# One fused kernel of attention and two expert layers: what a slot's two arms hold, and how the second layer's routing sums are laid out

## The chip, the cores and the metric

The kernel runs on one core of one Trainium2 chip. Times are device microseconds of one execution. The metric is the median of several runs; before the change it is 712.32 us over 3 runs (710.05 to 712.72). The engines are TensorE (PE, with its weight loads shown apart as PEld), VectorE (DVE), ScalarE (ACT), GpSimd (POOL) and SyncE (SP), and each has a sequencer that takes its instructions in program order (shown as PEldq, DVEq and so on).

## The reference

Three steps in a row, all in fp32. The first is a gated linear attention over 64-row blocks (4 batches, 8 heads, 768 rows of 64), whose output is 3072 tokens of 512. Then come two layers of experts: of eight experts each token takes the one with the largest gate, computes relu(x w1) w2 with w1 512x1024 and w2 1024x512, and scales it by its softmax weight. The second layer skips tokens whose skip score is not positive, and adds its input.

```python
def moe(x, w_gate, bias, w1, w2):
    logits = x @ w_gate + bias
    e_idx = argmax(logits, 1)
    gate_w = softmax(logits)[arange(N), e_idx]
    for e in range(8):
        mask = e_idx == e
        out[mask] = gate_w[mask, None] * (maximum(x[mask] @ w1[e], 0) @ w2[e])
    return out
x1 = moe(attention(q, k, v, lam), ...)
do = x1 @ w_skip > 0
x2 = x1.copy(); x2[do] = x1[do] + moe(x1[do], ...)
```

## The kernel before, in words

Tokens are written to a table, grouped by expert, and worked on in slots of 256 rows (two blocks of 128). Every fp32 product with the experts' weights is made of three faster ones: weights and inputs are split into a high and a low part (`w1h`, `w1l`, `xth`, `xtl`, `hh`, `hl`), and three matmuls are added up. ACT rounds the high parts, DVE subtracts to get the low ones.

The first expert layer has 14 slots (`which` = 0, kk = 0 to 13), the second 10 (`which` = 1). Slot kk = 0 of each is written out by itself (`first1`, `first2`). `slot` (L861 on) makes the others, `rec` nests them: the first twelve slots of layer 1 always run, each later one stands in an If of its own (`more0_12` and so on, L922), and their Else arm is the passage to the second layer (`tail`, L909).

A slot does two products, which the code calls `layer1` and `layer2`; in this document "step n" is the n-th output part of either. `layer1` (L710) is x w1: eight steps f of 12 matmuls with 256 columns each, at L717 to L719; behind every second step ACT takes relu (L724) and DVE the low part (L725). `layer2(j)` (L753) is h w2 for block j: eight steps n of three matmuls with 512 columns each, at L758 to L760. Both take functions to call behind a step (`steps`, `hooks`), which is how smaller work is laid between. `trans_x` transposes the next slot's rows (L350, copies at L353, low part at L354). `split_next` splits the next slot's w1 if its expert differs (flag `fl` > 0), with ACT at L304 and DVE at L305, and reloads the raw buffer (`fl` > 1). `split_w2` does the same for w2 at the head of a slot (L310, L311). Which expert, which flag and whether a slot is full is read by each engine from a table into a register (L323).

A slot with more than 128 rows is full; in a half one only block 0 has rows. `slot` decides by one If (L892), whose two arms each hold the whole rest of the slot: the full arm `layer1`, `trans_x`, `split_next` and both blocks; the half arm `layer1_half` (L729; rows as weights, w1 as 512 moving columns, L736 to L738, then transposes back, L745), `trans_x`, and block 0 with `split_next` behind its step 5. In this data three slots are half: kk = 6 and 12 of layer 1 and kk = 7 of layer 2. Each slot but the last ones of layer 1 also issues a prefetch hint for the next slot's branch (`ahead`, L864).

While slot kk of layer 1 runs, the 256 results of slot kk - 1 are routed for the second layer (`router`, L661; also once in `first2`). `tr` transposes them (L669) into `x2t`. `la` (L672) multiplies them with the gate weights `wgp`: the 512 inputs are cut in four parts c, and each part's product goes, without accumulation, to another 32 rows of a PSUM tile, 256 tokens wide; ACT copies that to `lgs` (L675). `lg` (L677) adds the four parts and turns the result to tokens in rows, by two matmuls with a 0/1 matrix `sel` (L679). `rk` (L681 on, DVE) finds the chosen expert per token as a 0/1 row `oh` and sums per expert. `rb` (L694 on) ranks the tokens by two small matmuls with `tri` and `ones` (L136, L137), turns that into table rows on DVE (L140 to L157) and scatters on POOL. In a full slot these are the steps 1 (`tr`), 3 (`la`), 4 (`lg`, `rk`) and 6 (`rb`) of `layer1`. In a half slot `la` stands behind the second half of `layer1_half`, `lg` and `rk` behind its DVE work, and `rb` in block 0.

Of the kernel before, what the change touches and what calls it, by code (L numbers as in the profile page):

```python
# [18 lines left out]
P = 128  # L19
E = 8  # L20
# [15 lines left out]
def body(ctx: ExitStack, tc: tile.TileContext, qkv, cpk, w1, w2, out, dbg=None):  # L36
# [77 lines left out]
    def route_a(L, n, mask=None):  # L114
        m = rt.tile([P, 4], F32, tag="m", name="m")
        nc.vector.tensor_reduce(out=m[:, :n], in_=L, axis=AX.X, op=ALU.max)
        d = rt.tile([P, 4, E], F32, tag="d", name="d")
# [5 lines left out]
        oh = rt.tile([P, 4, E], BF16, tag="oh", name="oh")  # L123
# [515 lines left out]
    lgs = hp.tile([P, 2, P], F32, name="lgs")  # L639
    wgp = hp.tile([P, 4, 32], F32, name="wgp")  # L640
    sel = hp.tile([P, E + 1], F32, name="sel")
    plg = pmi[:, 256:512].rearrange("p (j t) -> p j t", j=2)
# [11 lines left out]
    def fill():  # L654
        nc.gpsimd.memset(wgp, 0.0)
        nc.gpsimd.tensor_copy(out=wgp[:, :, 0:E + 1], in_=wgt2)
        nc.gpsimd.tensor_tensor(out=sel, in0=ident[:, 0:E + 1], in1=ident[:, 32:33 + E], op=ALU.add)
        for i in (64, 96):
            nc.gpsimd.tensor_tensor(out=sel, in0=sel, in1=ident[:, i:i + E + 1], op=ALU.add)
        for t in (x2r[1][1], xgm[0], xgm[1]):  # L660
            nc.gpsimd.memset(t, 0.0)  # L661

    def router(ix, kk=None):
        box = []
# [7 lines left out]
        def la():  # L672
            for c in range(4):
                nc.tensor.matmul(plg[32 * c:32 * c + 32], wgp[:, c], x2t[:, c], start=True, stop=True)
            nc.scalar.copy(out=lgs, in_=plg)  # L675

        def lg():  # L677
            for j in range(2):
                nc.tensor.matmul(pmi[:, 16 * j:16 * j + E + 1], lgs[:, j], sel, start=True, stop=True)  # L679

        def rk():  # L681
            L = rt.tile([P, 2, 16], F32, tag="L2", name="L2")
            nc.vector.tensor_copy(out=L[:, :, 0:E + 1], in_=pmi[:, 0:32].rearrange("p (t e) -> p t e", e=16)[:, :, 0:E + 1])
# [4 lines left out]
            mask = rt.tile([P, 2], F32, tag="mask", name="mask")  # L688
            nc.vector.scalar_tensor_tensor(out=mask, in0=L[:, :, E], scalar=0.0, in1=pres, op0=ALU.is_gt, op1=ALU.mult)
            oh, ex = route_a(L[:, :, 0:E], 2, mask)  # L690
            route_s(oh, 2, 1)
            box[:] = (oh, ex, mask)

        def rb(cnt=None):  # L694
            oh, ex, mask = box
# [12 lines left out]
        return tr, la, lg, rk, rb  # L708
# [110 lines left out]
    def first2():  # L819
        la, lg, rk, rb = router(itl)[1:]  # L820

        def arm(l1, js):
            tb = table(1)
            split_w2([0, 1])
            l1(0, {0: la, 1: lambda: (lg(), rk()), 3: lambda: rb(pcnt[1]), 5: lambda: (next(tb), split_w2([2, 3]))})
# [24 lines left out]
    def slots(which):  # L850
# [139 lines left out]
```

## Time and profile before

| | |
|---|---|
| median of 3 runs | 712.32 us (710.05 to 712.72) |
| the profiled execution | 719.15 us, span 717.1 us |
| mean granted clock of TensorE | 0.988 |
| busy: PE, PEld, DVE, ACT, POOL | 95%, 84%, 50%, 37%, 31% |
| DMA, mean | 153 GB/s, 109.82 MB |
| largest groups on PE | L717 to L719: 192.5, 187.7, 188.3 us; L758 to L760: 142.2, 141.5, 141.9 us |

The span runs from the first to the last instruction, and the execution's own time is a little longer. Matmuls overlap in their pipeline, so the busy time of a group on PE, and the sum of its durations, are more than what it adds: from the start of one matmul to the start of the next is what a step takes. "issue" marks time in which an engine waited for nothing that the profile shows.

### The profile page before, as it was taken

The numbers are of one execution on the slowest core, as the hardware profiler recorded it, in microseconds if no ns is written. First come the engines' busy times: TensorE is split into PE (matmuls) and PEld (weight loads), VectorE is DVE, ScalarE is ACT, GpSimd is POOL, SyncE is SP. The second block draws the span as 40 slices with busy tenths as digits, with TensorE's granted clock in tenths as the row PEclk, the third lists the DMA queues.
The fourth block names the chain that finished last, engine by engine and source line by source line (L and its number), as shares of the span: only waits on it lengthen the run. The fifth ranks groups of instructions, "written<-read, shape, count | busy, mean of one in ns | idle before, by whom it ended". The sixth has DMA issues, their size and how long they took to land. (4 is left out here: it accounts for less than half of the span.)

```text
span 717.1 us, 15677 instructions
## 1 busy us (share of the span) xinstructions
PE 681.1 (95%) x5348; PEld 603.1 (84%) x5348; DVE 360.9 (50%) x924; ACT 268.4 (37%) x476; POOL 221.5 (31%) x290
## 2 busy tenths in 40 slices
PE   6999999899999999999999999988999999979993
PEld 5889987778988998889889988776998899968992
DVE  5656676653303325843123327848227575675650
ACT  2444434522322226823223227432115545456530
POOL 4355656243221221533222233313121121202321
PEclk9999999999999999999999999999999999999998
DMA  8778866656230134782210211712715666755500
GB/s 272 234 199 223 231 180 195 205 154 260 90 116 31 62 120 164 234 308 91 90 46 22 90 63 48 259 61 63 277 59 183 214 199 235 240 193 179 193 17 28
DMA packets 60523, 109.82 MB, mean 153 GB/s; under 512 B 18656, under 2 KB 18784, under 8 KB 60368
## 3 DMA queue, kind: packets, MB, share of 16 engines
q1 hardware_dynamic: 48400, 86.65, 37.3%
q0 software_dynamic: 9744, 20.47, 8.6%
q8 instruction: 61, 1.00, 0.6%
q10 hardware_dynamic: 2224, 0.93, 0.6%
q14 instruction: 94, 0.77, 0.4%
HBM read 84.08 MB, written 30.06 MB: 159 GB/s over the span
## 5 line engine op out<-in xcount | busy, mean ns | idle before, releaser
L717 PE MATMUL p<-xth,w1h 128*128 128x256 f32 x672 | 192.5, 286 | 6.0 <-DVE itl L911 2.1
L719 PE MATMUL p<-xth,w1l 128*128 128x256 f32 x672 | 188.3, 280 | 0.2 <-DVE w1l L305 0.2
L718 PE MATMUL p<-xtl,w1h 128*128 128x256 f32 x672 | 187.7, 279 | 0.0
L725 DVE SCALAR_TENSOR_TENSOR hl<-p,hh 128x512 fp32r<-128x512 f32 x84 | 57.6, 690 | 175.0 <-ACT hh L724 149.4
L759 PE MATMUL p<-w2l,hh 128*128 128x512 f32 x360 | 141.5, 393 | 1.0 <-DVE w2l L311 0.8
L758 PE MATMUL p<-w2h,hh 128*128 128x512 f32 x360 | 142.2, 395 | 0.0
L760 PE MATMUL p<-w2h,hl 128*128 128x512 f32 x360 | 141.9, 394 | 0.0
L717 PEld LDWEIGHTS p<-xth,w1h 128*128 128x128 f32 x672 | 127.0, 189 | 13.0 <-issue 6.6
L160 POOL DMA_INDIRECT out_dram<-x2r,it x43 | 50.2, 1168 | 254.3 <-DVE x2r L771 102.6
L719 PEld LDWEIGHTS p<-xth,w1l 128*128 128x128 f32 x672 | 127.3, 189 | 1.5 <-DVE w1l L305 1.5
L718 PEld LDWEIGHTS p<-xtl,w1h 128*128 128x128 f32 x672 | 127.4, 190 | 0.9 <-DVEq L778 0.2
L724 ACT ACTIVATE hh<-p 128x512 fp32r<-128x512 f32 x84 | 50.3, 598 | 178.6 <-PE p L719 153.7
L759 PEld LDWEIGHTS p<-w2l,hh 128*128 128x128 f32 x360 | 67.7, 188 | 16.9 <-DVE w2l L311 2.5
L758 PEld LDWEIGHTS p<-w2h,hh 128*128 128x128 f32 x360 | 67.6, 188 | 14.0
L760 PEld LDWEIGHTS p<-w2h,hl 128*128 128x128 f32 x360 | 67.6, 188 | 13.9 <-DVE hl L725 0.3
L164 POOL DMA_INDIRECT xg<-xs,it x54 | 58.7, 1087 | 32.1 <-issue 18.5
L160 POOL DMA_INDIRECT tab<-pk,rows x28 | 31.0, 1108 | 102.0 <-issue 78.3
L311 DVE TENSOR_TENSOR w2l<-raw,w2h 128x1024 fp32r<-128x1024 f32 x48 | 55.9, 1220 | 8.3 <-ACT w2h L310 7.5
L768 ACT ACTIVATE x2r<-p,it 128x512 f32<-128x512 f32 x26 | 17.9, 689 | 102.5 <-PE p L760 92.9
L310 ACT CAST w2h<-raw 128x1024 fp32r<-128x1024 f32 x48 | 48.9, 1049 | 19.0 <-issue 12.4
L305 DVE TENSOR_TENSOR w1l<-raw,w1h 128x512 fp32r<-128x512 f32 x88 | 53.9, 684 | 0.4 <-ACT w1h L304 0.2
L304 ACT CAST w1h<-raw 128x512 fp32r<-128x512 f32 x88 | 47.0, 633 | 0.3 <-ACT ex L154 0.3
(217 smaller groups left out, 820.5 us busy)
## 6 DMA issues: line engine op xcount, KB each, us to landing
raw<-in_w_dram SPq DMA_DIRECT2D x96, 512.0 KB
kq<-in_qkv_dram SPq DMA_DIRECT2D x48, 256.0 KB
xs<-x2r SPq DMA_DIRECT2D x28, 256.0 KB
v<-in_qkv_dram SPq DMA_DIRECT2D x24, 256.0 KB
xs<-xr SPq DMA_DIRECT2D x24, 256.0 KB
xs<-xgm SPq DMA_DIRECT2D x7, 512.0 KB
xg<-xs,it POOLq DMA_INDIRECT x54
tab<-tini ACTq DMA_DIRECT2D x2, 416.0 KB
```

The source lines that it names most:

```text
L160: nc.gpsimd.indirect_dma_start(out=dst, out_offset=bass.IndirectOffsetOnAxis(ap=idx, axis=0), in_=rows, in_offset=None, bounds_check=dst.s ...
L164: return nc.gpsimd.indirect_dma_start(out=rows, out_offset=None, in_=src, in_offset=bass.IndirectOffsetOnAxis(ap=idx, axis=0), bounds_chec ...
L305: nc.vector.tensor_tensor(out=w1l[c][:, s], in0=raw1[:, c, s], in1=f32(w1h[c][:, s]), op=ALU.subtract)
L311: nc.vector.tensor_tensor(out=w2l[c], in0=r, in1=f32(w2h[c]), op=ALU.subtract)
L717: nc.tensor.matmul(o, w1h[c][:, fs], xh[:, c, :], start=(c == 0), stop=False)
L718: nc.tensor.matmul(o, w1h[c][:, fs], xl[:, c, :], start=False, stop=False)
L719: nc.tensor.matmul(o, w1l[c][:, fs], xh[:, c, :], start=False, stop=(c == 3))
L724: nc.scalar.activation(out=a, in_=pt, func=AF.Relu)
L725: nc.vector.scalar_tensor_tensor(out=b, in0=pt, scalar=0.0, in1=f32(a), op0=ALU.max, op1=ALU.subtract)
L758: nc.tensor.matmul(p2[j], a, w2h[g][:, i], start=(n == 0), stop=False)
L759: nc.tensor.matmul(p2[j], a, w2l[g][:, i], start=False, stop=False)
L760: nc.tensor.matmul(p2[j], b, w2h[g][:, i], start=False, stop=(n == 7))
```

## The change

Four things change.

1. **The arms.** The If of a slot holds layer 1 alone. Behind both arms stand once: `trans_x`, block 0 of layer 2 with `rb` behind step 3 and `split_next` behind step 5, and then a second If on the same flag. Its arm is block 1; for layer 1's slots its Else keeps the half slot's second block of rows.
2. **The routing sums.** `la` makes 16 matmuls: per part c of the inputs and per group n of 32 tokens of either block of 128, one of 64 columns into group n's 32 rows, accumulated over c. DVE then transposes blocks of 32x32 out of PSUM (L680 after), so `lgs`, `lg`, `sel` and POOL's three additions that built `sel` go.
3. **The order of routing.** `rk` stands at step 4 of layer 1 in full slots, and directly behind `la` in half ones; `rb` stands in block 0 for both. `oh`, `dd` and the mask lie in two fixed sets of buffers (`hold`), since `rb` is now outside the arm that made them.
4. **The hints.** Those for the full/half branches go; the one for leaving layer 1 stays and moves from step 5 of block 1 (step 6 of block 0 in a half slot) to step 1 of block 0.

```diff
-    def route_a(L, n, mask=None):
+    def route_a(L, n, mask=None, oh=None, d=None):
...
-    plg = pmi[:, 256:512].rearrange("p (j t) -> p j t", j=2)
+    plg = pmi[:, 256:320]
...
+    hold = [(hp.tile([P, 4, E], BF16, name=f"oh{i}"), hp.tile([P, 4, E], F32, name=f"dd{i}"),
+             hp.tile([P, 2], F32, name=f"mk{i}")) for i in range(2)]
...
     def router(ix, kk=None):
-        box = []
+        oh, ex, mask = hold[(kk or 0) % 2]
...
         def la():
             for c in range(4):
-                nc.tensor.matmul(plg[32 * c:32 * c + 32], wgp[:, c], x2t[:, c], start=True, stop=True)
-            nc.scalar.copy(out=lgs, in_=plg)
-
-        def lg():
-            for j in range(2):
-                nc.tensor.matmul(pmi[:, 16 * j:16 * j + E + 1], lgs[:, j], sel, start=True, stop=True)
+                for n in range(4):
+                    ns = slice(32 * n, 32 * n + 32)
+                    nc.tensor.matmul(plg[ns].rearrange("p (j t) -> p j t", j=2), wgp[:, c], x2t[:, c, :, ns],
+                                     start=(c == 0), stop=(c == 3))
 
         def rk():
-            L = rt.tile([P, 2, 16], F32, tag="L2", name="L2")
-            nc.vector.tensor_copy(out=L[:, :, 0:E + 1], in_=pmi[:, 0:32].rearrange("p (t e) -> p t e", e=16)[:, :, 0:E + 1])
+            L = rt.tile([P, 2, 32], F32, tag="L2", name="L2")
+            nc.vector.transpose(out=L.rearrange("p j e -> p (j e)"), in_=plg)
...
     def first2():
...
-            l1(0, {0: la, 1: lambda: (lg(), rk()), 3: lambda: rb(pcnt[1]), 5: lambda: (next(tb), split_w2([2, 3]))})
+            l1(0, {0: la, 1: rk, 3: lambda: rb(pcnt[1]), 5: lambda: (next(tb), split_w2([2, 3]))})
...
                     tc.mark_branch_hint_location(f"more0_{kk + 1}", hint=s_ > kk + 1, engines=FE)
-                elif kk + 1 < (NS1, NS2)[which]:
-                    tc.mark_branch_hint_location(f"full{which}_{kk + 1}", hint=full2, engines=FE)
...
-                steps = {1: lambda: tr(kk - 1, ptr), 3: la, 4: lambda: (lg(), rk()), 6: rb}
+                steps = {1: lambda: tr(kk - 1, ptr), 3: la, 4: rk}
...
-            with tc.If(full > 0, preferred_fallthrough_block=True, label=f"full{which}_{kk}") as c:
+            with tc.If(full > 0, preferred_fallthrough_block=True) as c:
                 layer1(kk, steps)
-                trans_x(which, kk + 1, ptr)
-                split_next(which, kk + 1, fl2)
-                layer2(which, kk, 0)
-                layer2(which, kk, 1, {5: ahead})
             with c.Else():
-                hooks = {6: ahead, 5: lambda: split_next(which, kk + 1, fl2)}
-                if which == 0:
-                    hooks[3] = rb
-                layer1_half(kk, {} if which else {1: steps[1], 3: la, 4: steps[4]})
-                trans_x(which, kk + 1, ptr)
-                layer2(which, kk, 0, hooks)
-                if which == 0:
+                layer1_half(kk, {} if which else {1: steps[1], 3: lambda: (la(), rk())})
+            trans_x(which, kk + 1, ptr)
+            hooks = {1: ahead, 5: lambda: split_next(which, kk + 1, fl2)}
+            if which == 0:
+                hooks[3] = rb
+            layer2(which, kk, 0, hooks)
+            with tc.If(full > 0, preferred_fallthrough_block=True) as c:
+                layer2(which, kk, 1)
+            if which == 0:
+                with c.Else():
                     keep(kk, 1)
             return fl2, full2
```

How it moves instructions, at three places (line numbers behind the change are the changed kernel's own).

PE, the end of the half arm's layer 1 in slot kk = 1, before: the four `la` products, transposes of the half's results, the `lg` products, `trans_x`, block 0.

```order
L737 MATMUL p_1881<-w1h_141,xtl_166 128x512
L738 MATMUL p_1881<-w1l_145,xth_164 128x512
L674 MATMUL pmi<-x2t,wgp 32x256 x4
L745 MATMUL p_1882<-ident,hrow_1868 128x128 x4
L745 MATMUL p_1878<-ident,hrow_1869 128x128 x4
L679 MATMUL pmi<-sel,lgs 128x9 x2
L350 MATMUL ptr_1879<-ident,xg_154 128x128 x4
L350 MATMUL ptr_1880<-ident,xg_155 128x128 x4
L758 MATMUL p_1883<-w2h_146,hh_1864 128x512
```

The same place behind the change:

```order
L731 MATMUL p_1879<-w1h_141,xtl_166 128x512
L732 MATMUL p_1879<-w1l_145,xth_164 128x512
L675 MATMUL pmi<-x2t,wgp 32x64 x16
L739 MATMUL p_1880<-ident,hrow_1868 128x128 x4
L739 MATMUL p_1876<-ident,hrow_1869 128x128 x4
L884 UNCONDITIONAL_BRANCH
L351 MATMUL ptr_1877<-ident,xg_154 128x128 x4
L351 MATMUL ptr_1878<-ident,xg_155 128x128 x4
L752 MATMUL p_1881<-w2h_146,hh_1864 128x512
```

`la` is now sixteen products of 64 columns, `lg` is gone, and the arm ends (L884) ahead of `trans_x`.

DVE, the half arm of the same slot, before: the low parts hl (L749), and behind them the head of `rk`.

```order
L986 BRANCH_PREFETCH_HINT
L749 TENSOR_TENSOR hl_1866<-p_1882,hh_1864 128x2x128 x2
L749 TENSOR_TENSOR hl_1867<-p_1878,hh_1865 128x2x128 x2
L683 COPY L_2706<-pmi 128x2x9
L685 CAST idf<-it_158 128x2
L687 TENSOR_SCALAR pres<-idf 128x2
L689 SCALAR_TENSOR_TENSOR mask<-L_2706,pres 128x2
```

Behind the change, from the end of `rk`'s chain on:

```order
L124 TENSOR_REDUCE sm<-sc 128x2
L125 TENSOR_TENSOR oh_1891<-sc,sm 128x16
L127 TENSOR_TENSOR oh_1891<-oh_1891,mk_1893 128x16
L133 TENSOR_TENSOR rs_121<-rs_121,oh_1891 128x8 x2
L743 TENSOR_TENSOR hl_1866<-p_1880,hh_1864 128x2x128 x2
L743 TENSOR_TENSOR hl_1867<-p_1876,hh_1865 128x2x128 x2
L884 UNCONDITIONAL_BRANCH
L355 TENSOR_TENSOR xtl_166<-ptr_1877,xth_164 128x4x128
L355 TENSOR_TENSOR xtl_166<-ptr_1878,xth_164 128x4x128
```

The chain of `rk` (it begins with L680, seven rows above) now stands ahead of hl (L743); hl is followed by the arm's end and the low part of the next x (L355).

PE, the end of a slot, before (half arm of slot kk = 1, with what each row waits for in brackets): the last matmul, the ends of the arms, the load of the next flag, the branch, the hint, the next slot.

```order
L760 MATMUL p_1883<-w2h_149,hl_1867 128x512
L778 UNCONDITIONAL_BRANCH
L892 UNCONDITIONAL_BRANCH
L878 UNCONDITIONAL_BRANCH
L323 TENSOR_LOAD ei_168
L892 COMPARE_AND_BRANCH
L986 BRANCH_PREFETCH_HINT
L717 MATMUL p_1878<-xth_164,w1h_138 128x256 [waits DVE_49,Activation_49]
```

Behind the change:

```order
L754 MATMUL p_1882<-w2h_149,hl_1867 128x512
L893 UNCONDITIONAL_BRANCH
L893 UNCONDITIONAL_BRANCH [waits PE_49]
L870 UNCONDITIONAL_BRANCH
L324 TENSOR_LOAD ei_168
L884 COMPARE_AND_BRANCH
L711 MATMUL p_1876<-xth_164,w1h_138 128x256 [waits Activation_49]
L712 MATMUL p_1876<-xtl_166,w1h_138 128x256 [waits DVE_49]
```

Between the last matmul and the flag's load stand block 1's end and the Else arm, which holds one wait for PE's own count; the hint is gone.

## Rows read from the trace of the kernel before

**Rows 1.** The page, part 1: busy time, share of the span, instructions.

```profile
PE 681.1 (95%) x5348; PEld 603.1 (84%) x5348; DVE 360.9 (50%) x924; ACT 268.4 (37%) x476; POOL 221.5 (31%) x290
```

**Rows 2.** Table by stretches, one full slot of layer 1; columns in its first line.

```profile
core 0: us, PE busy (x) PEld busy (x) DVE busy (x) ACT busy (x) POOL busy (x), PEclk, DMA share, GB/s
181.02:206.20 25.18, 25.18 (x176) 22.62 (x174) 6.84 (x26) 6.28 (x12) 6.41 (x9) 1.00 0.27 86
```

**Rows 3.** Timeline of PE in that slot: start, duration, instruction, [idle before].

```profile
187.48 0.64 PE L674 MATMUL pmi<-x2t,wgp 128*32 128x256 f32 x8
...
189.41 0.28 PE L719 MATMUL p<-xth,w1l 128*128 128x256 f32 x1
189.53 0.51 PE L679 MATMUL pmi<-sel,lgs 128*128 128x9 f32 x4
189.89 0.36 PE L717 MATMUL p<-xth,w1h 128*128 128x256 f32 x1
190.09 0.28 PE L718 MATMUL p<-xtl,w1h 128*128 128x256 f32 x1
```

**Rows 4.** Timeline of PE in the attention: two groups of small matmuls.

```profile
28.14 1.08 PE L371 MATMUL pmi<-xt,wgp 128*32 128x128 f32 x32
...
60.72 0.69 PE L552 MATMUL psK<-v,kd 128*64 128x64 f32 x16
```

**Rows 5.** Timeline of PE at layer 2's half slot.

```profile
639.67 0.40 PE L760 MATMUL p<-w2h,hl 128*128 128x512 f32 x1
644.25 0.76 PE L736 MATMUL p<-w1h,xth 128*128 128x512 f32 x1 [4.19 <-DVE w2l L311]
```

**Rows 6.** Timeline of the weight loads at the same place.

```profile
644.22 0.29 PEld L736 LDWEIGHTS p<-w1h,xth 128*128 128x128 f32 x1 [4.59 <-issue]
```

**Rows 7.** Table by stretches (columns as in rows 2): half arms, a slot's start, 644 on.

```profile
424.66:427.51 2.85, 2.85 (x14) 2.29 (x14) 2.24 (x14) 0.69 (x1) 1.38 (x2) 1.00 0.34 122
439.72:443.43 3.71, 3.71 (x26) 3.13 (x26) 3.71 (x7) 3.71 (x6) 2.98 (x3) 1.00 0.40 142
644.00:648.00 4.00, 3.75 (x9) 3.01 (x10) 1.57 (x2) 0.00 (x0) 2.06 (x2) 0.50 0.87 292
644.25:652.00 7.75, 7.75 (x24) 6.15 (x25) 1.32 (x2) 0.60 (x1) 3.09 (x3) 0.70 0.91 323
```

**Rows 8.** Timeline of DVE, then of PE, in the half slot of layer 1 at 424.7.

```profile
433.17 1.42 DVE L749 TENSOR_TENSOR hl<-p,hh 128x256 fp32r<-128x256 f32 x4 [5.80 <-ACT hh L746]
...
436.58 1.28 DVE L354 TENSOR_TENSOR xtl<-ptr,xth 128x512 fp32r<-128x512 f32 x2
...
439.26 4.92 DVE L305 TENSOR_TENSOR w1l<-raw,w1h 128x512 fp32r<-128x512 f32 x8 [0.22 <-ACT w1h L304]
...
431.80 1.09 PE L745 MATMUL p<-ident,hrow 128*128 128x128 f32 x8
...
433.92 0.47 PE L758 MATMUL p<-w2h,hh 128*128 128x512 f32 x1
```

**Rows 9.** The branch of L892 on PE's sequencer, ns min/median/max, 630:645, 415:428, 272:285.

```profile
L892 PEldq COMPARE_BRANCH  x2: 314/3795/7276, 635.8 to 636.7; - x2
L892 PEldq COMPARE_BRANCH  x2: 301/1296/2290, 420.5 to 422.0; - x2
L892 PEldq COMPARE_BRANCH  x2: 201/327/453, 277.6 to 278.3; - x2
```

**Rows 10.** Timeline of PE: where the ranking matmul waited.

```profile
294.24 0.17 PE L136 MATMUL pmi<-oh,tri 128*128 128x16 bf16 x1 [0.31 <-DVE oh L126]
...
454.44 0.17 PE L136 MATMUL pmi<-oh,tri 128*128 128x16 bf16 x1 [0.63 <-DVE oh L126]
```

**Rows 11.** Timeline of PE at the passage between the layers.

```profile
469.26 1.06 PE L350 MATMUL ptr<-ident,xgm 128*128 128x128 f32 x8 [1.06 <-issue]
...
473.27 0.36 PE L717 MATMUL p<-xth,w1h 128*128 128x256 f32 x1 [2.07 <-DVE itl L911]
```

**Rows 12.** The chain of waits ahead of 640: start, duration, what.

```profile
635.69 6.35 DMA raw<-in_w_dram
```

More of the change, by code (lines that the diff above doesn't have):

```diff
@@ L112, in body @@
     xtl = [wp.tile([P, 4, T], F32R, name=f"xtl{i}") for i in range(2)]
-    def route_a(L, n, mask=None):
+    def route_a(L, n, mask=None, oh=None, d=None):
         m = rt.tile([P, 4], F32, tag="m", name="m")
         nc.vector.tensor_reduce(out=m[:, :n], in_=L, axis=AX.X, op=ALU.max)
-        d = rt.tile([P, 4, E], F32, tag="d", name="d")
+        if d is None:
+            d = rt.tile([P, 4, E], F32, tag="d", name="d")
+            oh = rt.tile([P, 4, E], BF16, tag="oh", name="oh")
         nc.vector.tensor_tensor(out=d[:, :n], in0=L, in1=bc(m[:, :n].unsqueeze(2), [P, n, E]), op=ALU.subtract)
@@ L122, in route_a @@
         nc.vector.tensor_reduce(out=sm[:, :n], in_=sc[:, :n], axis=AX.X, op=ALU.max)
-        oh = rt.tile([P, 4, E], BF16, tag="oh", name="oh")
         nc.vector.tensor_tensor(out=oh[:, :n], in0=sc[:, :n], in1=bc(sm[:, :n].unsqueeze(2), [P, n, E]), op=ALU.is_equal)
@@ L638, in body @@
     x2t = hp.tile([P, 4, 2, P], F32, name="x2t")
-    lgs = hp.tile([P, 2, P], F32, name="lgs")
     wgp = hp.tile([P, 4, 32], F32, name="wgp")
-    sel = hp.tile([P, E + 1], F32, name="sel")
-    plg = pmi[:, 256:512].rearrange("p (j t) -> p j t", j=2)
+    plg = pmi[:, 256:320]
     p1 = [pp_.tile([P, 2, T], F32, name="p10")]
@@ L656, in fill @@
         nc.gpsimd.tensor_copy(out=wgp[:, :, 0:E + 1], in_=wgt2)
-        nc.gpsimd.tensor_tensor(out=sel, in0=ident[:, 0:E + 1], in1=ident[:, 32:33 + E], op=ALU.add)
-        for i in (64, 96):
-            nc.gpsimd.tensor_tensor(out=sel, in0=sel, in1=ident[:, i:i + E + 1], op=ALU.add)
         for t in (x2r[1][1], xgm[0], xgm[1]):
             nc.gpsimd.memset(t, 0.0)
+    hold = [(hp.tile([P, 4, E], BF16, name=f"oh{i}"), hp.tile([P, 4, E], F32, name=f"dd{i}"),
+             hp.tile([P, 2], F32, name=f"mk{i}")) for i in range(2)]
     def router(ix, kk=None):
-        box = []
+        oh, ex, mask = hold[(kk or 0) % 2]
         def tr(kk, ptr):
@@ L687, in rk @@
             nc.vector.tensor_scalar(out=pres, in0=idf, scalar1=float(OOB), scalar2=None, op0=ALU.is_lt)
-            mask = rt.tile([P, 2], F32, tag="mask", name="mask")
             nc.vector.scalar_tensor_tensor(out=mask, in0=L[:, :, E], scalar=0.0, in1=pres, op0=ALU.is_gt, op1=ALU.mult)
-            oh, ex = route_a(L[:, :, 0:E], 2, mask)
+            route_a(L[:, :, 0:E], 2, mask, oh, ex)
             route_s(oh, 2, 1)
-            box[:] = (oh, ex, mask)
         def rb(cnt=None):
-            oh, ex, mask = box
             rows = rt.tile([P, 2], U32, tag="rows2", name="rows2")
@@ L706, in rb @@
                 scatter(tabv[1][j], pk[:, j, :], rows[:, j:j + 1])
-        return tr, la, lg, rk, rb
+        return tr, la, rk, rb
     def layer1(kk, steps):
@@ L819, in first2 @@
     def first2():
-        la, lg, rk, rb = router(itl)[1:]
+        la, rk, rb = router(itl)[1:]
         def arm(l1, js):
```

2 lines of the change are left out of this document (1 added, 1 removed).

## The prediction

> **What bounds the kernel now.** I read the page's first part first: TensorE (PE) computes in 95% of the span [rows 1]. So I do not ask which engine is full but what PE does per slot, and where it stands still. A table by stretches gives one routed full slot of layer 1: 25.18 us, PE busy for all of it, at full granted clock [rows 2]. In such a slot only fewer PE instructions can save time; work on VectorE (DVE), ScalarE (ACT) and the queues lies beside PE. Then I listed PE's idle times with what ended them. In the slots that the change rewrites they are few: 4.19 us ahead of the half arm of layer 2 at 644.25 [rows 5], two short waits of the ranking matmul [rows 10], and 1.06 and 2.07 us at the passage between the layers [rows 11].
>
> **The routing sums (14 times).** Removed on PE are the two `lg` products, and four `la` products of 256 columns become sixteen of 64. Before, the `la` group shows 0.64 us. The `lg` group starts at 189.53 and the slot's own work resumes at 189.89, 0.36 later; the step from L717 to L718 behind it is 0.20, where a step takes 0.12 (189.41 to 189.53), so `lg` costs 0.44 to 0.45 [rows 3]. For the new `la` the trace has three neighbours. The old one, 0.64, streams the same columns through the same four groups of 32 rows. L552 (16 rows of 64 columns) shows 0.69. L371 shows 1.08, with the same 32 rows in the same four groups, but twice the columns [rows 4]. Columns explain 0.64 against 1.08, so I take 0.67, near both of the first two; the ends are 0.32 (half of 0.64, if the groups overlap better) and 1.08. Per full slot that gives 0.03 - 0.45 = -0.42; in the two half slots `lg` stands between transposes, with no longer step behind it, so 0.03 - 0.36 = -0.33. Twelve times 0.42 (the routing in first2 among them) and twice 0.33: **-5.7 us**, between -10.6 and 0. The ACT copy `lgs` that goes, and the DVE copy that becomes a transpose of 64 columns (at most an xtl piece, 0.64 [rows 8]), lie beside PE. If that cover goes, the ranking comes later by as much; it hides behind more than twelve matmuls, because `rb` now follows in block 0.
>
> **The ranking matmul (tri, ones).** In full slots it moves from step 6 of layer 1 into block 0 of layer 2, behind one more layer-1 step and trans_x. Its own cost is the same. Twice PE waited for DVE there, 0.31 and 0.63 us [rows 10]; with several us more between `rk` and `rb` that goes: **-0.9 us** (0 to -0.9).
>
> **The split of the next w1.** In full slots of layer 1 it moves from ahead of block 0 to step 5 of it, and on DVE behind the rest of `rb`, which waits for the ranking in step 3. On DVE's queue eight subtractions stand behind that wait, and on SP's the w1 load stands behind the split. The eight took 4.92 us [rows 8]. They begin some 4 us into block 0 instead of at its head and end after about 9; the next slot's layer 1 starts after about 11, as two blocks are 48 matmuls of some 0.23. Cost 0, hidden by block 1. Without that cover PE would lose about 1 us, as it does today after half slots, which have no block 1: its first 24 matmuls there took 3.71 us [rows 7], where 24 steps of 0.114 make 2.7. In layer 2 no `rb` stands between, and the order on ACT and DVE stays.
>
> **The half arms.** There are three: at 281.7, 424.7 and 644.25. At the last PE's timeline names DVE's w2l as what ended 4.19 us of idling, but no operand of L736 is w2l [rows 5], and the weight-load row says "issue" for the same gap: nothing that the profile shows was awaited [rows 6]. The rows of L892 show what PE's sequencer did: one COMPARE_BRANCH that began at 636.7 lasted 7.28 us, against 2.29 at 422 and 0.45 at 278 [rows 9]. It ended at 643.98, 0.24 before the first weight load at 644.22; PE's queued work had run out at 640.07, 3.4 us after the branch began. Afterwards PE worked at a granted clock of 0.50 from 644 to 648, the lower of its two levels (1.2 GHz): 24 matmuls took 7.75 us, while 12 took 2.85 in another half arm, so 5.70 for 24 [rows 7]. 4.19 + 2.05 = 6.24 us are at stake. In the changed kernel the layer-2 arm starts 193 instructions behind its branch (weight loads counted beside their multiplies), before 307; the layer-1 arms 273, before 352. I take the long branch to be a fetch of code that lay too far ahead, and expect it gone: -6.24.
>
> Here a rule speaks against the change: the Trainium skill, "Runtime: NRT & Kernel Launch", Instruction fetch mechanics, states that code streams in blocks of 256 instructions, two held, and that a taken branch to outside them stalls for a fetch. By that rule alone 193 is inside, and 273 may be outside for the layer-1 arms, without a prefetch hint now; what each would then cost is the slower rival's price. The trace does not bear it out in full: the branch at 422 had no hint before either, and cost PE nothing.
>
> The second If adds one branch per slot. On the usual path it is not taken, at some 0.2 to 0.3 us [rows 9], 3 to 4 us ahead of execution: 0. In a half slot PE's empty Else waits for PE's own last matmul (the order of instructions shows it). The sequencer then loads the next flag, branches (0.3) and starts the weights, behind 0.4 of the last matmul. The nearest idle time with nothing awaited is 1.06 [rows 11]; I take 0.9, ends 0 and 1.06. In layer 1's two half slots it hides, as the next slot there starts too early for its weights and loses that 1 us waiting for them. In layer 2 it counts once: +0.9. Together **-5.3 us** (1.06 to -6.24).
>
> In half arms `rk` now stands ahead of the four hl subtractions on DVE. Its chain took 2.0 us (434.59, the end of hl, to 436.58), and `la` ends at 431.80, so hl starts near 433.8 to 433.9 instead of 433.17 [rows 8]. Block 0's first use of hl comes some 0.5 us into the block, which itself starts 0.36 earlier than 433.92: 0.3 us of waiting, twice: **+0.6 us** (0 to 1.4).
>
> **The sum:** -5.7 - 0.9 - 5.3 + 0.6 = -11.3 us. The profiled execution took 719.15 us, so it would take 707.85. It is 6.8 us over the median of the runs, 712.32; I apply the sum to the median, which gives **701.0 us**.
>
> **The rivals.**
>
> *The 4 us wait stays, or is not in the timed runs.* The chain of waits goes through a 6.35 us weight transfer just ahead [rows 12] and the DMA engines were busy for 0.87 of 644 to 648 [rows 7]: the stall may be a transfer's, or one of the profiled execution alone, which is 6.8 us longer than the rest. Against it: L736 reads no w2. Then 712.32 - 5.7 - 0.9 + 0.6 + 0.9 = 707.2. Chance 0.18.
>
> *Sixteen small products cost what L371 costs.* If each of the 32 rows is paid by its weight load and not by its columns, `la` is 1.08: 0.41 more, 14 times, is 5.7, giving 706.7. L552's 16 rows in 0.69 speak for it a little; 0.64 against 1.08 speaks against. Chance 0.08.
>
> *Slower: the half arms wait without their hints.* If both layer-1 arms stall as the one at 644 did, and that one still does, the time is 707.2 + 2 x 6.24 = 719.7. It decides once the fetch outlasts the 3.4 us by which the sequencer leads. Against it: the unhinted branch at 422 took 2.29, the hinted one 7.28, and all arms are nearer now. Chance 0.06.
>
> *The passage between the layers gains too.* The hint for leaving layer 1 now stands at step 1 of block 0, a block earlier. If that brings the code in time, the 1.06 and 2.07 [rows 11] go: 697.9. Chance 0.12, as the 2.07 names DVE's copy of itl, which has its own chain.
>
> **How the numbers follow.** The forecast keeps 0.56. The range reaches down past the passage's gain, or to a `la` near its cheap end, and up past the two cases near 707 with 0.9 us of drain showing: 695.5 to 708.0. It leaves out the slower rival and the outer ends of the others, under 0.2. About 0.5% (3.6 us) is what a measurement of this kernel tells from no change, so faster means under 708.8. All cases but the slower rival lie there; of the two near 707 about a quarter could pass it. That gives faster 0.87, same 0.08, slower 0.05.
>
> **What would show it.** A `la` group with 32 rows of 0.6 to 0.7 us and no `lg`; full slots of layer 1 shorter by 0.4; no PE idle time over 1.5 us ahead of the layer-2 half arm, and 24 matmuls there in 5.7 us; branch rows under 3 us; no wait ahead of tri. I am wrong if a half arm starts after an "issue" gap, if PE waits for its weights by more than 1 us after a full slot, or if the `la` group nears 1 us.

## The result and the profile after

The changed kernel takes 703.17 us (median of 4 runs, 701.03 to 703.40) against 712.52 us of the kernel before on the same chip (4 runs, 710.05 to 715.78): 9.35 us less. The measured ratio is 0.9835, 95% interval 0.9800 to 0.9871. The ratios in this document are the measurement's own estimates and not quotients of the two medians beside them; this one stands for 11.8 us. The forecast was 701.0 with a range of 695.5 to 708.0. Measured again later (the change, once more, below), the ratio was 0.9882 (0.9832 to 0.9932). The profiled execution of the change took 703.4 us, span 701.7 us; that of before had taken 719.15 us, well over its median, and this matters below.

Part 1 of the page after:

```profile
PE 671.0 (96%) x5628; PEld 596.9 (85%) x5628; DVE 361.2 (51%) x924; ACT 262.5 (37%) x462; POOL 218.3 (31%) x287
```

TensorE is still the bound, busy for 10.1 us less than before (681.1), the work at a lower clock in [rows 7] included. The table by stretches (columns as in rows 2) shows a full slot of layer 1, the layer 1 part of two slots of the second layer, and the half arm of the second layer:

```profile
178.17:202.90 24.73, 24.73 (x196) 22.32 (x194) 6.84 (x26) 5.81 (x11) 6.42 (x9) 1.00 0.26 87
537.84:549.15 11.31, 11.31 (x97) 11.30 (x96) 7.31 (x8) 2.85 (x4) 3.09 (x3) 1.00 0.85 285
561.02:571.93 10.91, 10.91 (x97) 10.91 (x96) 7.27 (x8) 2.85 (x4) 3.37 (x3) 1.00 0.80 279
630.16:635.66 5.50, 5.50 (x26) 4.46 (x24) 5.29 (x5) 1.65 (x2) 0.03 (x1) 1.00 0.86 274
```

The full slot is 0.45 us shorter than in [rows 2]. Of the eleven full routed slots, nine are shorter by 0.38 to 0.50 us from start to start; the two behind half slots are shorter by 1.50 and 5.22, as waits went there (below). The half arm's 24 matmuls take 5.50 us at full clock, in place of the 7.75 of [rows 7]. The two rows between are the same 96 matmuls of the same kernel; one takes 0.40 us more. Before, such a slot of the second layer took the shorter time:

```profile
548.80:559.71 10.91, 10.91 (x97) 10.90 (x96) 7.37 (x8) 2.85 (x4) 3.64 (x3) 1.00 0.86 276
```

The new `la` group and what follows it, from PE's timeline, beside [rows 3]:

```profile
184.71 0.65 PE L675 MATMUL pmi<-x2t,wgp 128*32 128x64 f32 x32
185.29 0.39 PE L711 MATMUL p<-xth,w1h 128*128 128x256 f32 x1
```

It shows 0.65 us and holds the next matmul up by 0.58, as the old one did with 0.64 and 0.57. The rows of PE's timeline that have an idle time, in the parts that changed:

```profile
286.90 0.50 PE L754 MATMUL p<-w2h,hl 128*128 128x512 f32 x1 [0.32 <-DVE hl L743]
293.11 0.38 PE L711 MATMUL p<-xth,w1h 128*128 128x256 f32 x1 [0.73 <-ACTq L893]
427.09 0.50 PE L754 MATMUL p<-w2h,hl 128*128 128x512 f32 x1 [0.31 <-DVE hl L743]
432.91 0.17 PE L185 MATMUL pmi<-rs,ones 128*128 128x8 bf16 x1 [0.32 <-PEq L893]
434.23 0.38 PE L711 MATMUL p<-xth,w1h 128*128 128x256 f32 x1 [1.14 <-ACTq L893]
462.56 0.36 PE L711 MATMUL p<-xth,w1h 128*128 128x256 f32 x1 [1.59 <-DVE itl L902]
470.11 0.17 PE L137 MATMUL pmi<-oh,tri 128*128 128x16 bf16 x1 [0.92 <-DVE oh L127]
644.54 0.38 PE L711 MATMUL p<-xth,w1h 128*128 128x256 f32 x1 [0.94 <-PEq L893]
```

The 4.19 us ahead of the second layer's half arm [rows 5] and the two waits of [rows 10] are gone. New are the waits for hl in layer 1's half arms (0.32, 0.31), the waits behind each half slot's second If (0.73, 0.32 + 1.14, 0.94), and a wait of the ranking in first2 (0.92). At the passage the 1.06 of [rows 11] is gone, and the 2.07 is 1.59. Gone too is a wait of the kernel before that the forecast's list of idle times left out, though it is longer than the two of [rows 10]; it stood in the last slot of layer 1, in both traces of before (0.96 and 0.95):

```profile
452.16 0.38 PE L717 MATMUL p<-xth,w1h 128*128 128x256 f32 x1 [0.96 <-DVE hl L725]
```

The branches on PE's sequencer at the three half arms, and at the passage (one line's instructions, ns):

```profile
L884 PEldq COMPARE_BRANCH  x1: 759/759/759, 273.6 to 273.6; - x1
L884 PEldq COMPARE_BRANCH  x1: 327/327/327, 414.4 to 414.4; - x1
L884 PEldq COMPARE_BRANCH  x1: 346/346/346, 626.8 to 626.8; - x1
L913 PEldq COMPARE_BRANCH  x1: 1267/1267/1267, 455.2 to 455.2; - x1
```

None of them is long any more; before, they lasted up to 7.28 us [rows 9].

### The profile page after: what moved, and what is told of

Same layout as the page of the kernel before. It is cut to its first block, busy times and chain, and to the rows that moved or that the text cites. A ratio compares the mean times of both kernels' runs of the same rounds, so it can differ in the third digit from the quotient of the medians.

```text
span 701.7 us, 16337 instructions
## 1 busy us (share of the span) xinstructions
PE 671.0 (96%) x5628; PEld 596.9 (85%) x5628; DVE 361.2 (51%) x924; ACT 262.5 (37%) x462; POOL 218.3 (31%) x287
## 5 line engine op out<-in xcount | busy, mean ns | idle before, releaser
L711 PE MATMUL p<-xth,w1h 128*128 128x256 f32 x672 | 190.4, 283 | 6.3 <-ACTq L893 1.9
L752 PE MATMUL p<-w2h,hh 128*128 128x512 f32 x360 | 144.2, 401 | 0.0
L754 PE MATMUL p<-w2h,hl 128*128 128x512 f32 x360 | 141.5, 393 | 0.6 <-DVE hl L743 0.6
L161 POOL DMA_INDIRECT out_dram<-x2r,it x43 | 46.5, 1081 | 204.1 <-DVE x2r L765 101.6
L754 PEld LDWEIGHTS p<-w2h,hl 128*128 128x128 f32 x360 | 67.6, 188 | 16.5 <-DVE hl L743 1.5
```

The source lines that it names most:

```text
L161: nc.gpsimd.indirect_dma_start(out=dst, out_offset=bass.IndirectOffsetOnAxis(ap=idx, axis=0), in_=rows, in_offset=None, bounds_check=dst.s ...
L711: nc.tensor.matmul(o, w1h[c][:, fs], xh[:, c, :], start=(c == 0), stop=False)
L752: nc.tensor.matmul(p2[j], a, w2h[g][:, i], start=(n == 0), stop=False)
L754: nc.tensor.matmul(p2[j], b, w2h[g][:, i], start=False, stop=(n == 7))
```

## The experiments

**The kernel before, once more.** No edit; a second trace.

> The kernel before once more, for a second trace. Theory A (the 4.19 us wait ahead of layer 2's half arm belonged to that one profiled execution, which at 719.15 us was 6.6 us over its median): the time is near 712.5, the branch of L892 at that place lasts under 3.5 us, and PE's idle time ahead of L736 is under 1 us. Theory B (the wait is in every execution): the branch lasts about 7 us again, PE stands still for about 4 us, and the time is not over 716 all the same.

It took 715.91 us in its one run. From its trace: the branch, PE at the half arm of the second layer, and the 24 matmuls behind it (table by stretches).

```profile
L892 PEldq COMPARE_BRANCH  x2: 314/2955/5596, 635.8 to 636.7; - x2
```

```profile
642.56 0.47 PE L736 MATMUL p<-w1h,xth 128*128 128x512 f32 x1 [2.51 <-DVE w2l L311]
```

```profile
642.56:648.15 5.59, 5.59 (x24) 4.54 (x25) 3.00 (x3) 0.60 (x1) 2.19 (x3) 1.00 0.76 247
```

Neither theory holds as stated. The long branch is there again, but lasts 5.60 us instead of 7.28; PE stood still for 2.51 instead of 4.19, and this time the clock stayed at full. So the wait belongs to the kernel before, its size varies, and the first trace had shown a large one.

**The routing sums alone**, in the arms of before.

```diff
-                nc.tensor.matmul(plg[32 * c:32 * c + 32], wgp[:, c], x2t[:, c], start=True, stop=True)
-            nc.scalar.copy(out=lgs, in_=plg)
+                for n in range(4):
...
-                steps = {1: lambda: tr(kk - 1, ptr), 3: la, 4: lambda: (lg(), rk()), 6: rb}
+                steps = {1: lambda: tr(kk - 1, ptr), 3: la, 4: rk, 6: rb}
```

> The new routing sums alone in the kernel before (arms, hints and the order of rk and rb stay). Theory A: 14 times 0.42 to 0.45 us, so 5.7 to 6.3 us under before, near 706.5, and most of the change's 9.3. Rival (the gain comes from the arms, the sums move only work that lay beside PE): within 2 us of before.

716.03 us (10 runs) against 714.24 of before: a ratio of 1.0036 (1.0006 to 1.0066), slightly slower. The trace shows that both sides of this are real. A full slot, and the first half arm (table by stretches):

```profile
178.21:203.02 24.81, 24.81 (x196) 22.57 (x195) 6.85 (x26) 5.81 (x11) 6.44 (x9) 1.00 0.26 87
280.58:285.00 4.42, 4.42 (x13) 3.42 (x13) 3.40 (x3) 1.58 (x2) 2.93 (x2) 0.61 0.69 237
```

The slot is 0.37 us shorter than in [rows 2], as the sums should make it. But the sixteen products add 40 instructions to each arm (weight loads counted, two of each for an fp32 product, less what `lg` took), so that layer 1's half arms lie 392 to 394 instructions behind their branches instead of 352 to 354. The branches and PE's rows there:

```profile
L885 PEldq COMPARE_BRANCH  x2: 317/3256/6195, 273.3 to 274.1; - x2
L885 PEldq COMPARE_BRANCH  x2: 311/2162/4014, 418.2 to 419.8; - x2
L885 PEldq COMPARE_BRANCH  x2: 307/2591/4875, 636.7 to 637.6; - x2
```

```profile
280.58 0.47 PE L729 MATMUL p<-w1h,xth 128*128 128x512 f32 x1 [2.97 <-DVE w2l L311]
...
423.96 0.47 PE L729 MATMUL p<-w1h,xth 128*128 128x512 f32 x1 [1.50 <-DVE eb L198]
...
642.71 0.47 PE L729 MATMUL p<-w1h,xth 128*128 128x512 f32 x1 [1.77 <-ACT w2h L310]
```

All three half arms now wait. At the first, 2.97 us of standing and a granted clock of 0.61 behind it (4.42 us for 12 matmuls, 2.75 before) eat up the gain of eleven slots. So the sums give what was forecast, but not by themselves.

**The arms alone**, with the old sums, and rk behind hl in half arms.

```diff
-            with tc.If(full > 0, preferred_fallthrough_block=True, label=f"full{which}_{kk}") as c:
-                layer1(kk, steps)
-                trans_x(which, kk + 1, ptr)
...
+            with tc.If(full > 0, preferred_fallthrough_block=True) as c:
+                layer1(kk, steps)
+            with c.Else():
+                layer1_half(kk, {} if which else {1: steps[1], 3: la, 4: steps[4]})
+            trans_x(which, kk + 1, ptr)
```

> The arms of the change alone, with the old routing sums and rk behind hl in half arms. Theory A (half arms gain from the ranking moved to block 0, lose by the wait in PE's empty Else, layer 2's slots lose 0.4 us each by a slower step): 1 to 4 us under before, 708.5 to 711.5. Theory B (a 6.24 us wait goes): 5 to 8 us under before. Rival: the second If and the lost hints cost more than they bring, slower than before.

709.63 us (10 runs), ratio 0.9944 (0.9919 to 0.9969): 4.6 us less than before by the medians. The half arms' branches last 0.35, 0.33 and 0.22 us and none of them keeps PE waiting, but a full slot is longer than before by 0.17 us:

```profile
179.65:205.00 25.35, 25.35 (x175) 22.63 (x174) 6.84 (x26) 6.18 (x12) 6.40 (x9) 1.00 0.26 85
```

The break that the ranking makes costs about as much in block 0 as it did in layer 1, some 0.16 us by the starts of the matmuls around it. What is new is the step: all 72 layer-1 matmuls behind `tr` start 0.118 us apart, where before 48 of them started 0.114 apart. So the gain of this part comes from elsewhere. Beside the second trace of before, the half arm of the second layer with the slot ahead of it is 1.7 us shorter, PE's wait at the passage is 1.7 us shorter (1.72 for 3.39), and the waits of 0.95 and 0.62 us in the last slot of layer 1 are gone.

**The kernel before without its hints** for the full/half branches.

```diff
-                elif kk + 1 < (NS1, NS2)[which]:
-                    tc.mark_branch_hint_location(f"full{which}_{kk + 1}", hint=full2, engines=FE)
```

> The kernel before without the prefetch hints for the full/half branches, nothing else. If the hint costs the fetch that the next code needs (the hinted branches lasted 0.45 and 7.28 us, the unhinted one 2.29): the same as before or up to 3 us faster, and no branch of that line over 3 us. If the hints bring the half arms in time: up to 12 us slower, with PE idle for 2 to 6 us ahead of the half arms at 281 and 644.

722.03 us (4 runs), ratio 1.0132 (1.0074 to 1.0190): 7.8 us slower by the medians. The branch at the first half arm, 0.45 us with its hint [rows 9], and the one in the second layer:

```profile
L890 PEldq COMPARE_BRANCH  x2: 179/3579/6979, 273.4 to 274.0; - x2
L890 PEldq COMPARE_BRANCH  x2: 296/3398/6501, 639.5 to 640.4; - x2
```

```profile
281.17 0.76 PE L736 MATMUL p<-w1h,xth 128*128 128x512 f32 x1 [3.52 <-DVE w2l L311]
...
647.10 0.76 PE L736 MATMUL p<-w1h,xth 128*128 128x512 f32 x1 [3.30 <-DVE w2l L311]
```

The hint was worth all of 6.5 us at the first arm's branch. The mechanism of the slower rival was right for the kernel before.

**The change with the hints put back.**

```diff
+                elif kk + 1 < (NS1, NS2)[which]:
+                    tc.mark_branch_hint_location(f"full{which}_{kk + 1}", hint=full2, engines=FE)
```

> The changed kernel with the prefetch hints for the full/half branches put back (at step 1 of block 0). Theory C (what decides is how many instructions lie between the branch and the half arm: up to 273 the branch is short, from 307 on it lasts 2 to 7 us unless a hint came in time): the same as the change, 0.98 to 0.987 of before, no branch of that line over 1 us in either. Theory D (the change still loses time to the missing hints): 2 to 6 us faster than the change.

711.39 us (10 runs), ratio 0.9914 (0.9883 to 0.9944), against 0.9882 (0.9832 to 0.9932) for the change in a later session on another chip, and 0.9835 (0.9800 to 0.9871) in the first: no faster, so theory D falls. It was expected at 0.98 to 0.987, which it missed. The half arms' branches last 0.45, 0.33 and 0.22 us with hints and 0.76, 0.33 and 0.35 without.

**Block 0 back in the arms**, all else as in the change.

```diff
             with tc.If(full > 0, preferred_fallthrough_block=True) as c:
                 layer1(kk, steps)
+                trans_x(which, kk + 1, ptr)
+                layer2(which, kk, 0, hooks)
             with c.Else():
                 layer1_half(kk, {} if which else {1: steps[1], 3: lambda: (la(), rk())})
-            trans_x(which, kk + 1, ptr)
-            layer2(which, kk, 0, hooks)
+                trans_x(which, kk + 1, ptr)
+                layer2(which, kk, 0, hooks)
```

> The changed kernel with trans_x and block 0 of layer 2 back inside both arms; the second If, the routing sums and the missing hints stay, and the work done is the same. In layer 1 the half arm then lies 342 to 345 instructions behind its branch in place of 273, in layer 2 258 in place of 193. Theory C: the branch lasts 2 to 7 us at both half arms of layer 1, PE waits there for up to 3.6 us each, and stays short in layer 2; 2 to 7 us slower than the change, 705 to 710. Rival (the gain comes from merging itself, not from the distance): within 1 us of the change.

710.00 us (6 runs), ratio 0.9907 (0.9873 to 0.9941), not told apart by time from the change in its later session (0.9882). The three branches, and PE at the second half arm:

```profile
L887 PEldq COMPARE_BRANCH  x1: 419/419/419, 276.6 to 276.6; - x1
L887 PEldq COMPARE_BRANCH  x1: 4282/4282/4282, 420.0 to 420.0; - x1
L887 PEldq COMPARE_BRANCH  x1: 331/331/331, 635.2 to 635.2; - x1
```

```profile
424.40 0.47 PE L730 MATMUL p<-w1h,xth 128*128 128x512 f32 x1 [1.56 <-ACTq L870]
```

Of two branches over 342 and 345 instructions one is long and costs 1.56 us, the other is short: theory C was right about one arm of two. Counted over all programs of the study: 28 branches to half arms at most 274 instructions away all lasted under 1.0 us, with a hint or without; of 14 branches over 307 to 394 instructions, 11 lasted 2.3 to 7.3 us and three 0.42 to 0.45 us.

The traces show the fetch itself. Each of the 11 long branches ended 1.3 to 1.5 us after a 16 KB packet of a DMA queue for instructions had landed; in none of the 31 short ones did such a packet land while the branch lasted. For the branch of 7.28 us [rows 9] the packet began 4.8 us after the branch and landed 1.4 us before its end (DMA queues of the first trace of before, 636.72 to 643.99: packets, MB, share of 16 engines):

```profile
q8 instruction: 1, 0.02, 0.9%
```

The packet itself took 0.9 to 1.9 us; the rest of the difference is when it began. In six long branches the DMA engines were busy for 0.76 to 0.96 of the time until then, and it began 2.5 to 4.8 us after the branch; in the other five it began between 0.5 us before the branch and 1.0 us after it. That weight transfers held it up is a guess from this, and no run tests it. The first half arm of the change may be near the edge: its branch of 0.76 us, too, ended 1.5 us after such a packet had landed, one that had begun 2 us ahead of the branch.

**rk behind hl again**, in half arms of the change.

```diff
-                layer1_half(kk, {} if which else {1: steps[1], 3: lambda: (la(), rk())})
+                layer1_half(kk, {} if which else {1: steps[1], 3: la, 4: rk})
```

> The changed kernel with rk behind the hl subtractions again in half arms. By the trace of the change each of layer 1's two half arms then loses the 0.31 to 0.32 us wait for hl, and the ranking comes 0.4 us later, with no wait: 0.6 us faster than the change, not to be told from it by time; the trace decides: no wait of L754 for hl. Rival: the ranking matmul then waits instead, 0.3 us or more ahead of tri in both.

709.28 us (6 runs), ratio 0.9889 (0.9850 to 0.9929). Both waits of L754 for hl are gone; 0.14 us of a wait ahead of tri came at the first half arm. In exchange PE waited 0.80 us for hl in the last slot of layer 1, where the change has no wait, and the wait of the ranking in first2 was 2.19. And a wait for hh stood at the first half arm, in every one of the four kernels measured on that chip (2.09 to 2.52):

```profile
291.47 0.50 PE L752 MATMUL p<-w2h,hh 128*128 128x512 f32 x1 [2.52 <-ACT hh L740]
```

**The change, once more**, to see whether that wait is its own.

> The changed kernel once more, beside the version meant to beat it. In the four later kernels built on it PE waited 2.1 to 2.5 us at the first half arm for ACT (hh, L740), in the change's own trace 0.02. Theory E (that wait comes and goes with the execution or the chip, as ACT's code there is the same): it can show here too, and the time is 0.983 to 0.992 of before. Rival (the other kernels brought it in): no such wait, 0.980 to 0.987 of before.

709.07 us (6 runs, 703.75 to 712.20) against 716.46, ratio 0.9882 (0.9832 to 0.9932). The wait is there, though the program is the one whose first trace lacked it; ACT's timeline shows it. The wait of the ranking in first2 is 1.09 here.

```profile
289.06 0.50 PE L752 MATMUL p<-w2h,hh 128*128 128x512 f32 x1 [2.54 <-ACT hh L740]
...
475.90 0.17 PE L137 MATMUL pmi<-oh,tri 128*128 128x16 bf16 x1 [1.09 <-DVE oh L127]
```

```profile
284.14 0.60 ACT L733 ACTIVATE hrow<-p 128x512 f32<-128x512 f32 x1 [0.48 <-PE p L732]
288.43 1.07 ACT L740 CAST hh<-p 128x512 fp32r<-128x512 f32 x2 [3.69 <-remote]
```

So the wait comes and goes with the same program, as theory E has it. ACT stood for 3.69 us between two of its instructions in the half arm; in the first trace of the change the same gap was 0.57 us, the time that PE's transposes need. DVE stood there until the same moment, and it waits for PE's sums and not for ACT (this trace, then the first one of the change):

```profile
288.31 0.25 DVE L680 STREAM_TRANSPOSE L<-pmi 128x64 f32<-128x64 f32 x1 [4.28 <-remote]
284.28 0.25 DVE L680 STREAM_TRANSPOSE L<-pmi 128x64 f32<-128x64 f32 x1 [0.67 <-PE pmi L675]
```

Both engines wait for PE's semaphore, and the trace has its updates. PE's rows of the sums, the transposes and `trans_x` end from 284.63 to 286.53, but their five updates all came between 288.29 and 288.53, 0.06 us apart; in the first trace each came within 0.04 us of its row's end. No packet of an instruction queue moved during ACT's wait. So ACT and DVE waited for signals of PE that came late. The seven traces with this wait all show late signals of PE there, by 1.1 to 3.7 us at the first one. Why they came late stays open. Behind the 2.54 us PE also waited 1.11 us for hl, which came late with the rest.

**The hint for leaving layer 1 at its old place**, step 5 of block 1.

```diff
-            hooks = {1: ahead, 5: lambda: split_next(which, kk + 1, fl2)}
+            hooks = {5: lambda: split_next(which, kk + 1, fl2)}
-                layer2(which, kk, 1)
+                layer2(which, kk, 1, {5: ahead})
```

> The changed kernel with the hint for leaving layer 1 back at step 5 of block 1, where full slots had it before. If the earlier place is what shortened that branch (1.27 us in place of 3.0 to 4.7) and took away the 1.06 us wait ahead of the passage's transposes: the branch lasts over 3 us and up to 1.1 us come back. Rival: the branch stays near 1.3 us, and the time is that of the change.

710.63 us (10 runs), ratio 0.9932 (0.9898 to 0.9965) beside 0.9882 for the change in the same session. The branch, and PE at the passage:

```profile
L913 PEldq COMPARE_BRANCH  x1: 4814/4814/4814, 457.7 to 457.7; - x1
```

```profile
462.78 0.30 PE L351 MATMUL ptr<-ident,xgm 128*128 128x128 f32 x1 [1.21 <-issue]
...
467.36 0.39 PE L711 MATMUL p<-xth,w1h 128*128 128x256 f32 x1 [2.65 <-DVE itl L902]
```

The branch is long again, the 1.06 us of [rows 11] are back as 1.21, and the second wait is 2.65 where the change has 1.59. So the earlier hint is worth 1.2 + 1.1 = 2.3 us of PE's time: the two medians of that session differ by 1.6 us, and the intervals overlap.

**A version meant to beat the change**: rk behind hl, and in first2 the ranking one step later.

```diff
-            l1(0, {0: la, 1: rk, 3: lambda: rb(pcnt[1]), 5: lambda: (next(tb), split_w2([2, 3]))})
+            l1(0, {0: la, 1: rk, 4: lambda: rb(pcnt[1]), 5: lambda: (next(tb), split_w2([2, 3]))})
```

> A version meant to beat the change: rk behind hl in half arms, and rb of first2 behind step 4 in place of 3, where PE of the change waited 0.92 us ahead of tri for DVE. 0.6 + 0.9 = 1.5 us less than the change, near 0.982 of before. Rival: the wait moves to the next step and nothing is gained.

706.33 us (6 runs), ratio 0.9867 (0.9828 to 0.9907).

> The version with rk behind hl in half arms and rb of first2 one step later, again, on the same chip as the change. 1 to 1.5 us less than the change: 0.92 from the wait ahead of tri in first2, up to 0.6 from the two waits for hl. Rival: no difference above 0.5 us.

706.30 us (6 runs), ratio 0.9856 (0.9818 to 0.9895), beside 709.07 and 0.9882 of the change on the same chip: 2.8 us less by the medians, with intervals that overlap. In the trace the ranking in first2 follows without a wait, and no row of L754 waits for hl:

```profile
474.39 0.18 PE L137 MATMUL pmi<-oh,tri 128*128 128x16 bf16 x1
```

PE's wait for hh was there in both runs' traces (2.32 and 2.35 us), and so was the wait for hl in the last slot of layer 1 that rk behind hl brings (0.73 and 0.80).

**The same with ACT's code moved by 24 instructions.**

```diff
         fill()
+        for _ in range(24):
+            nc.scalar.copy(out=pad, in_=ident[:, 0:1])
```

> The version with rk behind hl and rb of first2 one step later, and 24 one-column copies on ACT added in first1, so that all of ACT's later code lies 24 instructions further on. Theory F (ACT's wait of 3.7 us in the first half arm is code that comes late where that arm happens to cross from one block of code to the next): with the crossing elsewhere PE does not wait for hh there, and the time is up to 2.4 us less than without the copies, 0.982 to 0.986 of before. Rival (it is the arm's own work or a transfer): PE waits 2 us or more for hh at the same place.

701.63 us (6 runs, 698.42 to 702.80) against 714.06 on its chip, ratio 0.9816 (0.9784 to 0.9848). PE's wait for hh is gone; ACT's timeline at that place, and the one wait for ACT that PE has instead, in the next full slot:

```profile
284.03 0.60 ACT L734 ACTIVATE hrow<-p 128x512 f32<-128x512 f32 x1 [0.48 <-PE p L733]
285.20 1.07 ACT L741 CAST hh<-p 128x512 fp32r<-128x512 f32 x2 [0.57 <-PE p L740]
```

```profile
300.69 0.32 PE L676 MATMUL pmi<-x2t,wgp 128*32 128x64 f32 x8 [0.80 <-ACT x2t L670]
```

With the 24 added instructions a wait of 2.3 us is gone and one of 0.80 us stands elsewhere, as theory F expected. It does not show theory F. The wait was absent from the first trace of the change too, without any copies; the seven traces that have it come from two chips, and this one trace from a third; and where it stands, PE's signals were late, for DVE as for ACT (above). Whether the copies or the execution took it away stays open. By the ratio to before on its own chip this is the fastest version of the study; it was not run on one chip with the change, and is not told apart from the change's first 0.9835.

## Why the prediction was right, and where it was not

The direction and the range were right. The sum was 11.3; the first measurement gave 9.35 by the medians and 11.8 by the ratio, the second 7.4 and 8.5. That the total comes so near is partly luck: the term of the half arms was too large by some 4 us, measured against the second trace of before, and gains that the sum did not have stand against it (below).

- **The routing sums, -5.7.** Right as a sum. `la` shows 0.65 us where 0.67 was taken, and a full slot is 0.45 us shorter where 0.42 was forecast. How the 0.45 comes about was not foreseen. The sums alone give 0.37, and the arms alone cost 0.17 (25.35 against 25.18), which would leave 0.2. The rest is a faster step: behind the new `la` the 48 layer-1 matmuls start on average 0.114 us apart, where in either part alone such stretches ran at 0.118.
- **The ranking, -0.9.** Both waits of [rows 10] are gone (the second trace of before has only the later one, 0.62). Its own cost is the same, as forecast: some 0.16 us of break in either place. In first2 a wait of 0.92 came up that the forecast did not look for: w2's split stands ahead of `rk` on DVE there.
- **The split of the next w1, 0.** Right: no full slot's start waits for a w1 piece.
- **The half arms, -5.3.** The mechanism was right, the size was off. Fetching code for a far branch was what PE waited for: each long branch ended 1.3 to 1.5 us after a packet of code had landed, and no branch over 274 instructions or fewer reached 1.0 us, with hints or without, while those over 307 to 394 lasted 2.3 to 7.3 us, except for a hinted one over 352 (0.45, in both traces of before) and one over 342 (0.42, with no hint). That the hint plays a part is shown by taking it away (0.45 became 6.98), and that the distance does, by block 0 put back (0.33 became 4.28 at one arm of two). What was mis-sized is the price that the timed runs pay: 6.24 us stood in the one trace that the forecast had, and from the start of the slot ahead to the end of the half slot that trace and the change's differ by 5.1 us (42.67 and 37.56); against the second trace of before (38.81) it is 1.25. The first trace's time, 719.15 against a median of 712.32, had said so, and the rival that gave it 0.18 named it; the forecast did not use it to lower the term. The other half of that rival, that the stall may be a transfer's, has something to it: the code is a DMA packet, and it came later where the engines were busy.
- **The rule that spoke against the change.** The Trainium skill, "Runtime: NRT & Kernel Launch", Instruction fetch mechanics, has code come in blocks of 256 instructions with two held. The traces agree with it: long branches only at 307 and more, none at 274 and less, and at 342 and 345 one of each kind, as it would be if it matters where in its block a branch stands (no run moved a branch within its block to show that). The two arms that it might have put outside, 273 behind their branches, were short in every trace.
- **The drain behind half slots, +0.9.** Measured 0.94 in the second layer. In layer 1, 0.73 and 0.32 + 1.14 show, and the slots behind them then start without waiting for their weights (24 matmuls in 2.92 and 2.84 us, where the first trace of before has 3.98 and 3.71): hidden but for 0.3 us or so, as forecast.
- **rk ahead of hl, +0.6.** Measured 0.32 + 0.31. In the four traces of the change with rk back behind hl they are gone, and 0.73 to 0.80 us of waiting for hl stands in the last slot of layer 1.
- **The rivals.** The passage's gain came in part, though it was given only 0.12: the 1.06 went and 0.5 of the 2.07, by the earlier hint, as the run with the hint at its old place shows (the second trace of before has the two in one, 3.39; the change 1.59 in both traces). The dear `la` did not come. The slower rival's mechanism exists, and costs the kernel before 7.8 us when its hints go; it does not reach the change, because the arms came nearer.
- **Not in the forecast.** In four of the second layer's slots the 96 matmuls of layer 1 took 0.40 us more than before, 1.6 us in all. Against them stand gains that the sum lacks: from the start of layer 1's second half slot to that of the second layer's first slot, the second trace of before takes 48.82 us and the change 45.39, 3.4 less, of which 1.8 is the wait at the passage and 0.95 the wait for hl that the list left out; and 2.0 us lie ahead of slot kk = 1, where the change does next to nothing. The second trace of the change has waits of 2.54 and 1.11 us behind late signals of PE, the first none; the runs of this kernel spread from 701 to 712 us, where the forecast took one trace for the kernel.

## What to carry to other kernels

An edit's gain in the steady state and the place where it puts the code are two effects, and the second can eat the first: shorten what lies between a branch and its target first, then change the work in the arms, and count instructions as the sequencer does. Before a stall of one trace goes into a sum, set that execution's time against the other runs; if it is higher by about the stall, the stall is worth less. A wait that names an engine long done, with "issue" on the weight loads, is a question to the sequencers' rows and to the packets of the instruction queues. Before a gap is put down to one engine's code, look at what else waits for the same signal: here DVE stood as long as ACT.

## What was not expected of the hardware

The layer-1 matmuls (256 columns, full granted clock) run at one of two steps, 0.1135 or 0.118 us, and keep to one for a whole stretch: 96 take 10.91 or 11.31 us with the same instructions, and PE has no idle row in either. In the second layer's full slots the two traces of the change agree on which one each slot got, and the two of before do but for the first slot and the one behind the half slot (11.31 and 10.91 us). What stands ahead does not decide it: behind the transposes of `tr` the step was 0.1135 before and 0.118 in the change, behind the new `la` it was 0.118 with the sums alone and 0.1135 in the change. Its cause stays open; no experiment was made on it.

Behind PE's idle time of 2.51 us the next 24 matmuls ran at full granted clock (2.4 GHz). Behind 2.97 and 3.52 us the granted clock was 0.61 and 0.62 over the 12 matmuls that followed, and behind 3.30 us it was 0.64 over 24, a mix of the two levels, 1.2 and 2.4 GHz; 24 matmuls took 8.39 us there and 5.50 at full clock.

The stall of a far branch has its packet in the trace: 16 KB on an instruction queue, landed 1.3 to 1.5 us before the branch ends, in all 11 cases.

PE's signals can come late by up to 3.7 us while its own rows show nothing: in one execution of the change five of them came bunched within 0.24 us, ACT and DVE stood until then, and in another execution of the same program each came on time. ACT's row names "remote" for it, as does DVE's. The cause stays open.
